# Retention with a gated feed-forward: transposing four chunks' activations by DMA, and a longer hand-ordered end

## The chip, the cores and the metric

The kernel runs on one core of a Trainium2 chip. The core has five engines with a queue each: TensorE (PE, matmuls; PEld is its weight load), VectorE (DVE), ScalarE (ACT), GpSimd (POOL) and SyncE (SP), which here issues nearly all transfers. An engine works its queue strictly in order; an instruction that waits keeps all behind it waiting. Sixteen DMA engines carry out the transfers. The metric is the device time of one execution in microseconds (us), lower being better. Three runs of the kernel before took 215.89, 216.18 and 216.53 us, a median of 216.18 us.

## The reference

Eight sequences of 576 positions with 8 heads of 64 go through a retention layer (attention with a decaying mask and no softmax), and the 4608 resulting rows of 512 through a feed-forward layer.

```python
scores = scale * np.matmul(q, k.transpose(0, 1, 3, 2))
ret = scores * Dmat[None]              # gamma_h ** (i - j) for i >= j, else 0
x = np.matmul(ret, v)                  # -> rows of 512
h = x @ w_in                           # 512 -> 1024
e = np.exp(h - h_max); sm = e / (e.sum(-1) + 1e-9)
solu = h * sm
ln = (solu - mu) / np.sqrt(var + 1e-6) * g_ln
out = ln @ w_out                       # 1024 -> 512
```

The inputs q, k, v and the weights are 32-bit; the kernel multiplies in 16-bit.

## The kernel before, in words

The work is cut into 36 chunks of 128 rows, numbered 0 to 35. Nine chunks belong to a pair of sequences: four chunks of 128 positions of each, alternating, and a last one (chunks 8, 17, 26 and 35) that holds the 64 remaining positions of both. From chunk to chunk of one sequence a state (keys times values, decayed) is carried, so the scores are only needed inside a chunk.

Each step of a chunk is a small function with a name of two letters:

- `ld` loads q, k and v of a chunk (three transfers on SyncE; six for chunks 8, 17, 26, 35). `cq`, `ck`, `cv` turn them into scaled 16-bit copies; the letter behind the chunk names the engine (a ScalarE, v VectorE, g GpSimd).
- q and k must be transposed for the scores. `tr` transposes on TensorE into a PSUM bank, and `er` copies the result out. From chunk 12 on, `tr` does only q (4 transposes), and `kd` has the keys transposed by a DMA on SyncE; the last chunks of the pairs are excepted (`chunks[n][1] == 4`): for them `kd` does nothing and `tr` transposes q and k (8 transposes, the group `tp`). `kq` transposes q by DMA, for one chunk.
- `sc` makes the scores (two banks), `mk` masks them on VectorE, `kv`, `ad`, `d3`, `dk` carry the state, `av` and `fs` make the retention output x, `ex` copies it out of PSUM.
- `m1` is the first projection (16-bit, eight matmuls of 512 columns, tile h), `mx` its row maximum (VectorE), `xp` the exponential (ScalarE), `so` the product u (VectorE), `sq` the sum of squares (ScalarE), `rt` the inverse root (three small POOL instructions).
- u must be transposed for the second projection. `tu` does this with eight transposes on TensorE into a bank (tile lp) and `eu` copies it out; `du` has a DMA do it instead, on SyncE, from SBUF to SBUF.
- `m2` is the second projection (eight matmuls of 512 columns, tile o), `st` scales its result on ScalarE and stores it through SyncE.
- The last chunk, 35, is done in halves by `hm`, `hx`, `hp`, `ho`, `ht`, `he`, `hq`, `h2`, `hw`.

The order of all queues is written out by hand, as lists of `step:chunk:engine`: START with absolute chunk numbers, LOOP relative to the loop's index i, END relative to chunk 35 (so `du:-7` is chunk 28). The steps are issued in the order of the lists, and each engine's queue is the order in which its steps occur there. LOOP runs for i from 7 to 27, and its steps reach from `tu`, `eu`, `sq`, `rt`, `m2`, `st` of chunk i-2 to `ld` of chunk i+6. A step that doesn't apply to its chunk does nothing.

`BANKS` names, for every PSUM tile that a step takes in turn, which of four banks it uses; two more pairs of banks hold h. SBUF tiles rotate over fixed numbers of buffers: five for u and for its transposed copy uT, four for qkT (the transposed q and k), seven for the loaded q and v, six for the loaded k.

So the program's order, the bank list and the buffer counts set when what can start; nothing is planned at run time.

Of the kernel before, what the change touches and what calls it, by code (L numbers as in the profile page):

```python
# [20 lines left out]
PLAIN = 5  # L21
FIRST = 7
STEP = 1
STOP = 28
BY_DMA = 12
START = """
ld:0 ld:1 c1:0 ck:0:g cq:0:v cv:0:v li:3 gt:0 c2:0 tq:0 cq:1:g cv:1:v ld:2 kv:0 ck:1:v tq:1 ad:0
# [17 lines left out]
ex:1:a rt:-2 cq:4:g xp:0 m2:-2 d3:0 ck:5:g st:-2 mk:2  # L45
"""
END = """
d3:-7 tr:-5 kd:-3 cq:-3:g kv:-6 av:-6 er:-5:v ld:-1 ad:-6 tr:-4 fs:-6 ex:-6:a dk:-7 sq:-9
so:-8 sc:-5 m1:-7 cv:-4:g er:-4:v mk:-5 tr:-3 kd:0 kv:-5 ck:-2:g av:-5 sq:-8 fs:-5 tu:-8 mx:-7
ad:-5 rt:-9 cv:-3:g dk:-5 er:-3:a tu:-9 kd:-2 m1:-6 xp:-7 sc:-4 kv:-4 cq:-2:v eu:-9:v so:-7  # L50
ex:-5:a m1:-5 sc:-3 mk:-4 rt:-8 du:-7 d3:-6 ld:0 mx:-6 eu:-8:a d3:-5 mk:-3 ad:-4 ck:-1:a dk:-6
m2:-9 av:-4 mx:-5 xp:-6 kv:-3 av:-3 d3:-4 cv:-1:g st:-9 d3:-1 ad:-3 kd:-1 cv:-2:g d3:-2 cq:0:g
fs:-4 fs:-3 so:-6 tr:-2 er:-2:v ex:-4:a xp:-5 m2:-8 sq:-6 dk:-4 sc:-2 mk:-2 ck:0:g m1:-4 so:-5
kv:-2 kv:-1 du:-5 ex:-3:a av:-2 sq:-7 st:-8 mx:-4 sq:-5 xp:-4 fs:-2 m1:-3 cq:-1:v cv:0:g kq:-1
rt:-5 dk:-3 ex:-2:a d3:-3 ad:-2 du:-6 tr:0 so:-4 er:0:a m2:-7 sc:0 m1:-2 ad:-1 mk:0 mx:-3
sc:-1 rt:-6 mk:-1 mx:-2 m2:-5 sq:-4 du:-4 kv:0 rt:-7 rt:-4 av:-1 av:0 fs:-1 dk:-1 m2:-6 st:-7
xp:-3 so:-3 ex:-1:v xp:-2 so:-2 du:-3 du:-2 dk:-2 sq:-3 st:-6 fs:0 m1:-1 rt:-3 ex:0:a st:-5
sq:-2 hm:0:0 hm:0:1 m2:-3 mx:-1 hx:0:0 hx:0:1 xp:-1 hp:0:1 so:-1 m2:-2 hp:0:0 ho:0:1 ho:0:0
du:-1 ht:0:1 hc:0 st:-3 ht:0:0 m2:-4 he:0:1:v sq:-1 hq:0:0:v he:0:0:v rt:-2 rt:-1 ad:0
hq:0:1:a h2:0:0 rt:0 m2:-1 h2:0:1 st:-4 st:-2 hw:0:0:a st:-1 hw:0:1:v  # L60
"""

BANKS = """
012312012012302130312031321320132103123120132130123012301230123012301230213021320132012301230213
021320132012301230213021320132013201321032103120312013201321032103120312013201321032103120312031
203102310210321032120312310213230213210213023201203203
"""


# [22 lines left out]
def kernel(  # L92
# [33 lines left out]
    chunks = []  # L126
# [4 lines left out]
    NCH = len(chunks)  # L131
# [29 lines left out]
    def bank(shape, dtype, name):  # L161
        return ps.tile(shape, dtype, tag="b" + next(banks), name=name)
# [4 lines left out]
    def copy(engine, out, in_):  # L167
        (engine.copy if engine is nc.scalar else engine.tensor_copy)(out=out, in_=in_)  # L168
# [32 lines left out]
    def tq(n):  # L201

        tp = bank([P, 2, 4, P], F16, "tp")
        for i, src in enumerate((T.pop(("q16", n)), T["k16", n])):
            s2 = src.rearrange("p h d -> p (h d)")
            for hp in range(4):
                nc.tensor.transpose(  # L207
                    out=tp[:, i, hp], in_=s2[:, hp * P : (hp + 1) * P], identity=ident
                )
        T["tp", n] = tp  # L210

    def kd(n):
        if chunks[n][1] == 4 or n < BY_DMA:
            return
        T["qkT", n] = att.tile([P, 2, 4, P], F16, name="qkT", bufs=4)
        nc.sync.dma_start_transpose(
            out=T["qkT", n][:, 1], in_=T["k16", n].rearrange("p h d -> p (h d)")
        )
# [4 lines left out]
        )  # L223

    def tr(n):
        if chunks[n][1] == 4 or n < BY_DMA:
            return tq(n)
        tp = bank([P, 4, P], F16, "tr")
        s2 = T.pop(("q16", n)).rearrange("p h d -> p (h d)")
        for hp in range(4):  # L230
            nc.tensor.transpose(  # L231
                out=tp[:, hp], in_=s2[:, hp * P : (hp + 1) * P], identity=ident
            )
        T["tp", n] = tp

    def er(n, e="a"):
        if chunks[n][1] == 4 or n < BY_DMA:
            return eq(n, e)
        copy(ENG[e], T["qkT", n][:, 0], T.pop(("tp", n)))

    def eq(n, e="v"):

        qkT = att.tile([P, 2, 4, P], F16, name="qkT", bufs=4)
        tp = T.pop(("tp", n))
        for i, x in enumerate(e if len(e) > 1 else ()):
            copy(ENG[x], qkT[:, i], tp[:, i])
        if len(e) == 1:
            copy(
                ENG[e], qkT.rearrange("p a b c -> p (a b c)"), tp.rearrange("p a b c -> p (a b c)")
            )  # L250
        T["qkT", n] = qkT
# [453 lines left out]
    def run(order, base):  # L705

        for token in order.split():
            name, n, *more = token.split(":")
            n = base + int(n)
            if 0 <= n < NCH:  # L710
                step[name](n, *more)

    with tc.manual_schedule():
        run(START, 0)
        for i in range(FIRST, STOP - STEP + 1, STEP):
            run(LOOP, i)
# [31 lines left out]
```

## Time and profile before

| What | Value |
|---|---|
| median of three runs | 216.18 us |
| profiled execution | 215.92 us, of which span 214.2 us |
| TensorE busy | 197.2 us (92%) |
| VectorE, ScalarE, GpSimd busy | 172.6, 166.3, 174.5 us |
| granted TensorE clock, mean | 0.998 |
| DMA | 47.04 MB, mean 220 GB/s |
| chain that ended last | PE 70%, DVE 12%, SPq 11% |

The span runs from the first to the last instruction; the time of an execution has some 1.7 us more. "SPq" in the chain is SyncE's queue. In the slices of the span a digit is the busy tenth of a fortieth of the span, some 5.4 us. The busy time of TensorE is modelled at the matmuls' ends, so a full TensorE is one that always has a matmul under way. Transfers are shown with their issue on SyncE (start and length) and, by group, with the time from issue to landing.

### The profile page before, as it was taken

Reading aid. Unit: us, or ns where it says so; the run is one execution under the profiler, and the core shown is the slowest. Engines: PE = TensorE matmul, PEld = TensorE weight load, DVE = VectorE, ACT = ScalarE, POOL = GpSimd, SP = SyncE. Lnnn points to the kernel's source line nnn. Section 1 sums busy time; section 2 is a strip of 40 time slices with the busy share of each in tenths; the row PEclk is TensorE's granted clock in tenths of the full one; section 3 lists DMA queues with packets and bytes.
Section 4 is the critical chain, followed back from the end, with each engine's and each line's share of the span. In section 5 each row is a group of like instructions: output and inputs, shape, how many; then the busy total and the mean of one; then the engine's idle time right before and its main releaser. Section 6 shows DMA issues by size and latency. Waiting matters only on the chain.

```text
span 214.2 us, 5359 instructions
## 1 busy us (share of the span) xinstructions
PE 197.2 (92%) x1989; PEld 110.5 (52%) x1989; DVE 172.6 (81%) x284; ACT 166.3 (78%) x269; POOL 174.5 (81%) x275
## 2 busy tenths in 40 slices
PE   1369888999999999999999999999999999999993
PEld 0244455555555555555555555555555565445451
DVE  1278999999997888888887888888878999879840
ACT  2073896989898888888888888888888776967991
POOL 3329799699997899999997899999988999897440
PEclk9999999999999999999999999999999999999999
DMA  7999999999999999899999999799999989792745
GB/s 148 258 291 292 195 221 355 232 187 229 275 282 247 257 200 197 180 254 242 240 224 232 244 206 198 177 258 232 232 227 227 238 170 206 168 196 78 196 115 180
DMA packets 139130, 47.04 MB, mean 220 GB/s; under 512 B 132824, under 2 KB 133088, under 8 KB 139104
## 3 DMA queue, kind: packets, MB, share of 16 engines
q1 hardware_dynamic: 138784, 46.55, 99.6%
q8 instruction: 15, 0.25, 0.5%
q10 hardware_dynamic: 320, 0.16, 0.4%
q14 instruction: 11, 0.09, 0.1%
HBM read 32.53 MB, written 9.44 MB: 196 GB/s over the span
## 4 chain that ended last, share of the span: by engine, by line
PE 70%; DVE 12%; SPq 11%; DMA 2%; issue 2%; POOL 1%; DVEq 0%; POOLq 0%
PE o L485 25%; PE h L382 22%; SPq L177 10%; PE lp L465 5%; PE sc L260 4%; PE x L350 3%; PE x L335 3%; PE kp L284 3%; DMA qf<-in_q_dram 2%; PE tr L231 2%; DVE u L407 2%; DVE nm L392 2%; DVE ret L273 2%; DVE w_c L700 2%; SPq L656 1%
## 5 line engine op out<-in xcount | busy, mean ns | idle before, releaser
L382 PE MATMUL h<-w_in,xT 128*128 128x512 f16 x264 | 62.4, 379 | 0.5 <-DVE u L407 0.5
L485 PE MATMUL o<-w_c,uT 128*128 128x512 f16 x240 | 56.5, 379 | 0.2
L398 ACT ACTIVATE e<-h,nm 128x1024 f32<-128x1024 f32 x35 | 39.0, 1116 | 11.5 <-DVE nm L392 11.5
L273 DVE TENSOR_TENSOR ret<-sc,tris 128x512 f16<-128x512 f32 x72 | 46.0, 680 | 1.3 <-PE sc L260 1.2
L407 DVE SCALAR_TENSOR_TENSOR u<-h,e 128x1024 f16<-128x1024 f32 x35 | 42.7, 1220 | 2.3 <-ACT e L398 0.9
L392 DVE TENSOR_REDUCE nm<-h 128x1 f32<-128x1024 f32 x35 | 42.4, 1214 | 2.1 <-PE h L382 2.0
L485 PEld LDWEIGHTS <-uT 128*128 128x128 f16 x280 | 26.2, 98 | 26.9
L382 PEld LDWEIGHTS <-xT 128*128 128x128 f16 x264 | 24.2, 98 | 24.5 <-issue 0.5
L184 POOL TENSOR_TENSOR v<-vf,small 128x512 f16<-128x512 f32 x32 | 33.4, 1044 | 3.4 <-DMA vf<-in_v_dram 3.4
L435 ACT ACTIVATE sq<-u,su 128x1024 bf16<-128x1024 f16 x30 | 34.7, 1158 | 0.2 <-DVE u L407 0.2
L184 POOL TENSOR_TENSOR q<-qf,small 128x512 f16<-128x512 f32 x30 | 31.8, 1061 | 3.5 <-DMA qf<-in_q_dram 3.5
L311 POOL TENSOR_TENSOR s<-t,small 128x512 f16<-128x512 f32 x32 | 33.8, 1058 | 0.0
L168 ACT CAST xT<-x 128x512 f16<-128x512 f32 x34 | 19.9, 586 | 11.4 <-PE x L350 10.9
L493 ACT ACTIVATE o_sb<-o,rs 128x512 f32<-128x512 f32 x35 | 23.9, 684 | 4.3 <-POOL rs L457 2.3
L168 ACT COPY uT<-lp 128x1024 f16<-128x1024 f16 x25 | 25.3, 1011 | 0.3 <-PE lp L465 0.2
L457 POOL TENSOR_TENSOR rs<-w,mhalf 128x1 f32<-128x1 f32 x36 | 19.9, 553 | 3.0
L168 POOL CAST k<-kf 128x512 f16<-128x512 f32 x28 | 17.4, 623 | 3.4 <-DMA kf<-in_k_dram 3.4
L299 DVE TENSOR_TENSOR t<-kp,s 128x256 f32<-128x256 f32 x24 | 10.1, 420 | 12.5 <-POOL s L311 10.2
L453 POOL TENSOR_SCALAR w<-ss,w 128x1 f32<-128x1 f32 x31 | 8.3, 267 | 14.1 <-ACT sq L435 11.8
L168 ACT COPY qkT<-tp 128x1024 f16<-128x1024 f16 x10 | 10.0, 1013 | 9.7 <-PE tp L207 9.7
L465 PE MATMUL lp<-ident,u 128*128 128x128 f16 x224 | 16.9, 219 | 0.7 <-DVE u L423 0.7
L323 POOL TENSOR_TENSOR s<-t,small 128x256 f32<-128x256 f32 x24 | 14.9, 621 | 2.6 <-DVE t L297 2.6
(88 smaller groups left out, 260.0 us busy)
## 6 DMA issues: line engine op xcount, KB each, us to landing
qf<-in_q_dram SPq DMA_DIRECT2D x32, 256.0 KB, 4.2
kf<-in_k_dram SPq DMA_DIRECT2D x32, 256.0 KB, 4.7
vf<-in_v_dram SPq DMA_DIRECT2D x32, 256.0 KB, 4.8
out_dram<-o_sb SPq DMA_DIRECT2D x32, 256.0 KB, 2.7
w_in<-in_moe_w_in_dram SPq DMA_DIRECT2D x4, 512.0 KB, 5.2
w_out<-in_moe_w_out_dram SPq DMA_DIRECT2D x4, 512.0 KB, 6.3
qf<-in_q_dram SPq DMA_DIRECT2D x8, 128.0 KB, 3.8
kf<-in_k_dram SPq DMA_DIRECT2D x8, 128.0 KB, 3.8
```

What stands on the lines that cost most here:

```text
L168: (engine.copy if engine is nc.scalar else engine.tensor_copy)(out=out, in_=in_)
L184: engine.tensor_tensor(out=dst, in0=T.pop((key, n)), in1=table.unsqueeze(2).to_broadcast([P, H, D]), op=ALU.mult,)
L273: nc.vector.tensor_tensor(out=r, in0=s, in1=m, op=ALU.mult)
L311: nc.gpsimd.tensor_tensor(out=s16, in0=t.unsqueeze(2).to_broadcast([P, 4, 2, D]), in1=gd.unsqueeze(3).to_broadcast([P, 4, 2, D]), op=ALU.mult,
L382: nc.tensor.matmul(out=h[:, i * 512 : (i + 1) * 512], lhsT=xT[:, d], rhs=w_in16[:, d, i * 512 : (i + 1) * 512], start=d == 0, stop=d == 3,)
L392: nc.vector.tensor_reduce(out=nm, in_=T["h", n], axis=AX.X, op=ALU.max, negate=True)
L398: nc.scalar.activation(out=e, in_=T["h", n], func=ACT.Exp, bias=T.pop(("nm", n)), accum_out=s)
L407: nc.vector.scalar_tensor_tensor(out=u, in0=T.pop(("h", n)), scalar=-1.0, in1=T.pop(("e", n)), op0=ALU.mult, op1=ALU.mult, accum_out=su,)
L435: nc.scalar.activation(out=s, in_=T.pop(("v", n)), func=ACT.Square, scale=-float(DFF), bias=T.pop(("su", n)), accum_out=ss,)
L465: nc.tensor.transpose(out=lp[:, c], in_=u[:, c * P : (c + 1) * P], identity=ident)
L485: nc.tensor.matmul(out=o, lhsT=uT[:, c], rhs=w[:, c], start=c == 0, stop=c == NF - 1)
L493: nc.scalar.activation(out=o_sb, in_=T.pop(("o", n)), func=ACT.Copy, scale=T.pop(("rs", n)))
```

## The change

LOOP stops at i = 23 instead of 27, and its four last passes become part of a new END. There, u of chunks 24 to 27 is transposed by `du` and no longer by `tu` and `eu`. The exception for the last chunks of the pairs shrinks to chunk 35, so that the keys of chunks 17 (in LOOP) and 26 are transposed by DMA too. The new END has another order on all engines: among other things the load of chunk 31 stands ahead of that of chunk 30, `er` of chunks 26 to 31 and 33 runs on ScalarE instead of VectorE, three `cv` go from GpSimd to VectorE, and two `ck` from GpSimd to ScalarE. BANKS is written anew to fit.

```diff
-STOP = 28
+STOP = 24
@@ END (the first and last lines of each; numbers relative to chunk 35)
-d3:-7 tr:-5 kd:-3 cq:-3:g kv:-6 av:-6 er:-5:v ld:-1 ad:-6 tr:-4 fs:-6 ex:-6:a dk:-7 sq:-9
...
-hq:0:1:a h2:0:0 rt:0 m2:-1 h2:0:1 st:-4 st:-2 hw:0:0:a st:-1 hw:0:1:v
+d3:-10 so:-12 cv:-8:g kd:-7 tu:-13 ld:-4 kv:-9 tr:-8 ad:-9 m1:-11 sq:-13 kv:-10 ad:-10 cq:-7:g
+tr:-9 eu:-13:a er:-8:a av:-10 fs:-10 dk:-10 er:-9:a mx:-11 tu:-12 sc:-9 mk:-9 ex:-10:a rt:-13
+cv:-7:g eu:-12:a xp:-11 kv:-8 m1:-10 sq:-12 ck:-6:a ad:-8 tr:-7 dk:-11 er:-7:a so:-11 sc:-8
+du:-11 m2:-13 av:-9 cv:-6:g ld:-5 sc:-7 mk:-8 fs:-9 mx:-10 cq:-4:g kd:-6 ck:-4:g m2:-12
+cq:-6:v st:-13 sq:-11 mk:-7 av:-8 ex:-9:a fs:-8 kd:-4 rt:-11 xp:-10 ex:-8:v cq:-5:g kv:-7
+so:-10 cv:-4:g tr:-6 m1:-9 er:-6:a ck:-5:a av:-7 rt:-12 d3:-8 m2:-11 m1:-8 mx:-9 cv:-5:g fs:-7
+sc:-6 xp:-9 kv:-6 dk:-8 ld:-3 kd:-5 tr:-5 ex:-7:a ad:-7 d3:-11 so:-9 dk:-7 mx:-8 st:-12
+cq:-3:g cv:-3:g st:-11 mk:-6 du:-10 m1:-7 er:-5:a ld:-2 ad:-6 av:-6 fs:-6 dk:-6 xp:-8 so:-8
+ex:-6:a du:-9 d3:-7 tr:-4 er:-4:a sc:-5 tr:-3 ck:-3:g mk:-5 mx:-7 m1:-6 mx:-6 sq:-10 kd:-3
+kv:-5 ld:-1 er:-3:a rt:-10 cq:-2:g av:-5 kv:-4 xp:-7 fs:-5 ad:-5 so:-7 ex:-5:a d3:-6 m2:-10
+sc:-4 ck:-2:g ad:-4 ad:0 m1:-5 du:-7 xp:-6 mk:-4 kd:-2 sq:-7 so:-6 tr:-2 dk:-5 av:-4 sq:-9
+kv:-3 er:-2:a d3:-5 du:-8 fs:-4 ad:-3 d3:-4 rt:-9 mx:-5 m2:-9 ld:0 ex:-4:a ck:-1:v cq:-1:g
...
+hw:0:0:v st:-1 hw:0:1:v
@@ in kd, tr and er alike
-        if chunks[n][1] == 4 or n < BY_DMA:
+        if n < BY_DMA or n == NCH - 1:
```

More of the change, by code (lines that the diff above doesn't have):

```diff
@@ L47 @@
 END = """
-d3:-7 tr:-5 kd:-3 cq:-3:g kv:-6 av:-6 er:-5:v ld:-1 ad:-6 tr:-4 fs:-6 ex:-6:a dk:-7 sq:-9
[L49 to L59, printed above, removed]
@@ new lines @@
+kv:-3 er:-2:a d3:-5 du:-8 fs:-4 ad:-3 d3:-4 rt:-9 mx:-5 m2:-9 ld:0 ex:-4:a ck:-1:v cq:-1:g
+sc:-3 sq:-6 kd:-1 mk:-3 sq:-8 kq:-1 cv:-1:v cv:-2:v xp:-5 d3:-3 m1:-4 m2:-7 rt:-7 dk:-4 st:-10
+rt:-8 sc:-2 mx:-4 du:-6 mk:-2 st:-9 m2:-8 av:-3 cq:0:g fs:-3 kv:-1 ck:0:g kv:-2 kd:0 dk:-3
+d3:-9 rt:-6 st:-7 xp:-4 av:-2 so:-5 fs:-2 tr:0 st:-8 ex:-3:a so:-4 du:-5 ex:-2:a ad:-2 er:0:a
+cv:0:v ad:-1 m1:-3 sq:-5 dk:-1 sc:0 mx:-3 sc:-1 mk:-1 m1:-2 rt:-5 dk:-9 sq:-4 m2:-6 mk:0 kv:0
+xp:-3 du:-4 av:0 mx:-2 so:-3 dk:-2 av:-1 fs:0 ex:0:a fs:-1 ex:-1:v du:-3 xp:-2 so:-2 m2:-5
@@ L61 @@
+sq:-3 m1:-1 st:-6 hm:0:0 hm:0:1 st:-5 mx:-1 sq:-2 rt:-2 m2:-4 xp:-1 hx:0:0 d3:-1 hx:0:1 hp:0:0
+m2:-3 so:-1 ho:0:0 hp:0:1 ho:0:1 du:-2 ht:0:0 rt:-3 ht:0:1 hc:0 m2:-2 du:-1 he:0:0:v rt:-4
+st:-4 hq:0:0:v hq:0:1:a he:0:1:v sq:-1 st:-2 rt:0 h2:0:0 m2:-1 d3:-2 st:-3 h2:0:1 rt:-1
+hw:0:0:v st:-1 hw:0:1:v
 """
 BANKS = """
-012312012012302130312031321320132103123120132130123012301230123012301230213021320132012301230213
-021320132012301230213021320132013201321032103120312013201321032103120312013201321032103120312031
@@ L66 @@
-203102310210321032120312310213230213210213023201203203
+012312012012302130312031321320132103123120132310323210321301230123012301320132031203123012301320
+132031203123012301320132031203120312032103210231023120312032103210231023120312031023120310231203
+23021330213021302102120203120312132020130123012012
 """
@@ L225, in tr @@
     def tr(n):
-        if chunks[n][1] == 4 or n < BY_DMA:
+        if n < BY_DMA or n == NCH - 1:
             return tq(n)
@@ L236, in er @@
     def er(n, e="a"):
-        if chunks[n][1] == 4 or n < BY_DMA:
+        if n < BY_DMA or n == NCH - 1:
             return eq(n, e)
```

## The prediction

> **What bounds the kernel now.** I read the page first: busy shares, slices, the chain that ended last.
>
> ```profile
> span 214.2 us, 5359 instructions
> PE 197.2 (92%) x1989; PEld 110.5 (52%) x1989; DVE 172.6 (81%) x284; ACT 166.3 (78%) x269; POOL 174.5 (81%) x275
> PE   1369888999999999999999999999999999999993
> PEclk9999999999999999999999999999999999999999
> DMA  7999999999999999899999999799999989792745
> q8 instruction: 15, 0.25, 0.5%
> PE 70%; DVE 12%; SPq 11%; DMA 2%; issue 2%; POOL 1%; DVEq 0%; POOLq 0%
> ```
>
> From 60 us to 210 us TensorE has no free slice, its granted clock is full, and the chain lies on it. So TensorE work that goes is time saved, as long as nothing else holds TensorE up. The chain in order of time gives the price of such work, and the end.
>
> ```profile
> 147.22 0.45 PE tp L207 x8
> 158.06 0.45 PE lp L465 x8
> 172.66 0.98 PE lp L465 x16
> 209.63 0.89 PE oh L589 x8
> ```
>
> Eight transposes are 0.45 us of TensorE; the last matmul ends at 210.52 us, and 3.7 us of eviction and store follow. The change lays work on SyncE's queue, so I read that queue in order of time.
>
> ```profile
> 151.07 0.43 SPq L177 DMA_DIRECT2D qf<-in_q_dram  x1
> 151.55 0.70 SPq L177 DMA_DIRECT2D kf<-in_k_dram  x1
> 152.29 1.03 SPq L177 DMA_DIRECT2D vf<-in_v_dram  x1
> 153.50 1.47 SPq L216 DMA_TRANSPOSE qkT<-k  x1
> 155.06 0.52 SPq L498 DMA_DIRECT2D out_dram<-o_sb  x1
> ...
> 156.96 2.30 SPq L177 DMA_DIRECT2D vf<-in_v_dram  x1
> ...
> 168.70 3.04 SPq L216 DMA_TRANSPOSE qkT<-k  x1
> 171.84 0.53 SPq L498 DMA_DIRECT2D out_dram<-o_sb  x1
> ...
> 177.52 1.25 SPq L470 DMA_TRANSPOSE uT<-u  x1
> 178.81 1.32 SPq L177 DMA_DIRECT2D qf<-in_q_dram  x2
> ```
>
> Columns are start, duration, instruction. One issue starts where the last ends: between 151 and 186 us SyncE waits for nobody, and its stores go out 1.5 to 2.9 us after ScalarE made them. SyncE is full, not only TensorE; its delay is hidden because loads run chunks ahead. The last view is of the engines that take what SyncE brings.
>
> ```profile
> 178.28 0.62 ACT L168 CAST k<-kf 128x512 f16<-128x512 f32 x1 [2.73 <-DMA kf<-in_k_dram]
> 183.99 1.04 POOL L184 TENSOR_TENSOR q<-qf,small 128x512 f16<-128x512 f32 x1 [0.95 <-DMA qf<-in_q_dram]
> 185.97 0.61 POOL L168 CAST k<-kf 128x512 f16<-128x512 f32 x1
> 188.27 0.39 PE L207 MATMUL tp<-ident,k 128*128 128x128 f16 x4
> ```
>
> The brackets are idle time. Only the loads of chunks 34 and 35 are placed by END now, and both were waited for. TensorE transposes chunk 35 (q from 188.05 us, then this k) 1.5 us after its keys were cast: that is all the slack left.
>
> **The change, part by part.** *TensorE.* Four `tu` go: 4 x 0.45 = 1.8 us. `tr` of chunks 17 and 26 halves: 2 x 0.22 = 0.44 us. Together -2.2 us, all on the path.
>
> *Other engines, behind the loop.* By row durations ScalarE loses three copies of `lp` (3 x 1.01) and one key cast (0.62), `ex` of 27 (0.58) and a half eviction (0.47), and takes seven `er` (7 x 0.57) and two key casts (1.24): +0.5 us. VectorE loses seven `er` (0.42 each, 0.69 for 26) and an `lp` copy (0.68), nets one `cq` less (0.69), and takes three `cv`, one `ck`, one `ex` and the half eviction: -0.9 us. POOL nets two `ck` and three `cv` less and one `cq` more: -3.3 us. All have 12 to 22% idle, and TensorE's 100% covers them. Uncovered, an `er` queued behind an exponential on ScalarE can keep the scores waiting: between 0 and 1.0 us (the exponential's own waits there are 0.8 to 0.9). I take 0, since the queue below is later than any of it.
>
> *SyncE.* Added: `kd` of 17 and 26, `du` of 24 to 27. From the start of chunk 30's load (151.07) to that of chunk 35's (178.81) the queue now issues 5 loads, 6 `kd`, 4 stores and 1 `du` in 27.74 us. Start to start these are: load 2.17 to 3.80 us, mean 2.62; `kd` 1.27 to 3.14, mean 1.83; store 0.60; `du` 1.29. The new order has, from `kd` of 28 to the load of 35: kd 28, ld 31, du 24, ld 30, kd 29, st 22, kd 31, ld 32, kd 30, st 23, st 24, du 25, ld 33, du 26, kd 32, ld 34, du 28, kd 33, du 27. That is 5 loads, 6 `kd`, 3 stores, 5 `du`: 27.74 - 0.60 + 4 x 1.29 = 32.3 us. It begins 1.55 us later, at 152.6, for `kd` of 26 now stands ahead of it. So the load of 35 starts at 184.9 us, not 178.8.
>
> What waits for it: the second half of q is issued 0.70 us later and needs 3.8 us to land (the page's median of such halves), then POOL scales q (1.04) and casts k (0.61): 191.1 us. `tr` of 35 needs both, and behind it on TensorE stand, in both orders, nine groups of eight 512-column matmuls and the same small ones; before, they took from 188.05 to 210.52. It moves by 191.1 - 188.05 = +3.0 us, and so does the end. The 2.2 us saved lie ahead of this wait and are eaten by it. TensorE is held up earlier on the same queue: `du` of 27 starts at 183.6 and lands 3.1 us later, 186.7; its `m2` (1.73) and six small groups (1.4) come before `tr` of 35, which puts that at 189.8, +1.8 by itself.
>
> *Ends.* Not shown before: how SyncE issues this mix. Shortest durations throughout (load 2.17, `kd` 1.27, store 0.56, `du` 1.29) bring the load of 35 at 178.9; middle ones (2.43, 1.55, 0.57, 1.29) at 182.3, +0.4 us; means, +3.0. Upward, `kd` of 17 also pushes SyncE by 1.55 us at 96 us; a transposed key lands 1.6 to 3.9 us before its scores in the loop, so TensorE does not feel it there, but what is left of the push at 151 us is between 0 and 1.55. I take the means, which are this queue's own under this load, and 0 for `kd` of 17, because the store's delay falls back to 0.5 to 0.8 us after each push by a six-transfer load.
>
> The long issues (2.30, 3.04) coincide with the 16 KB packets of the instruction queue, which start at 156.9 and 170.1 us; 180.5 and 193.6 follow. The Trainium skill ("Runtime: NRT & Kernel Launch", Instruction fetch mechanics) says crossing a 16 KiB block of instructions costs one DMA tail-bump, mostly hidden. By that no long issue belongs in the sum, and the middle durations' +0.4 us would hold; the trace has them on every such packet since 146 us, so I keep them.
>
> **Rivals.** *SyncE keeps up (faster).* If issues run near their shortest, the load of 35 starts before 181.2 us, POOL is done before TensorE gets there, and the saved transposes count: 216.18 - 2.2 = 214.0 us, up to 215.0 if the evictions on ScalarE bite. For it: 6.3 us of the old stretch (172.5 to 178.8) ran at 1.27, 2.17, 1.55, 1.29. Against: no stretch of 25 us did. It decides at the load of 35: started at 181.9, `tr` of 35 stands where it stood; each us is a us.
> The Trainium skill ("DMA: Bandwidth & Descriptors", Issuing engines are not separate DMA queues) says the sequencer's time to initiate a DMA is usually small relative to the DMA itself, by which four more would hardly delay the rest, and this rival's 214.0 would hold. Here a `du` holds SyncE 1.25 us of its 3.1.
>
> *A draw.* Middle durations, +0.4 us: 216.6, between 215.5 and 216.8. The long issues speak against it.
>
> *Worse (part of slower).* With `kd` of 17 still unabsorbed, +4.6: 220.8 us.
>
> **How the numbers follow.** The profiled execution took 215.92 us: span 214.2 and 1.7 around it, 0.26 below the median of 216.18. 214.2 + 3.0 + 1.7 = 218.9 on that footing, 219.2 on the median. Chances: forecast with its worse variant 0.67, draw 0.11, SyncE keeps up 0.22. 0.3% is 0.65 us, about what a measurement of this kernel can tell from no change; slower 0.67, same 0.11, faster 0.22. The forecast's own range is 216.9 to 221.2. The whole range reaches down to 214.8, inside the faster case, and leaves out the rest of it (0.13) and 0.05 above.
>
> **What would show it.** Right: on SyncE the load of chunk 35 starts after 182 us; POOL's `qf` wait before chunk 35 grows from 0.95 us; TensorE shows idle before `tp` of 35 and before `m2` of 27, its busy time down 2 us with the span up; ScalarE or POOL waits for chunk 30's load, which now stands behind chunk 31's. Wrong: that load starts before 181 us, or TensorE is solid to the end, and the span is near 212.

## The result, and the profile after

| What | Before | After |
|---|---|---|
| median | 216.09 us (4 executions) | 223.32 us (4 executions, 222.45 to 224.27) |
| ratio | 1 | 1.0333, 95% interval 1.0279 to 1.0386 |
| profiled execution, span | 215.92, 214.2 us | 223.94, 222.2 us |
| moved by DMA | 47.04 MB | 48.35 MB |

Ratios and intervals leave out executions more than 1.5% above the fastest one of their kernel.

The kernel became 7.2 us slower; the forecast was 3.0 us. The direction and the queue were as forecast, the size was not, and 223.32 lies above the range's 221.2. First the page of the changed kernel: span, busy shares, four rows of the slices, the instruction packets, the chain.

```profile
span 222.2 us, 5280 instructions
PE 196.8 (89%) x1949; PEld 108.4 (49%) x1949; DVE 173.3 (78%) x281; ACT 166.8 (75%) x272; POOL 171.7 (77%) x271
...
PE   1379889988999999999999999899997889997993
...
PEclk9999999999999999999999999999999999999999
DMA  7999999999999996999999896999999989789635
...
q8 instruction: 15, 0.25, 0.5%
...
PE 36%; SPq 16%; DMA 15%; POOL 14%; ACT 6%; DVE 6%; issue 6%; POOLq 0%; ACTq 0%
```

The 40 removed transposes are gone (1989 to 1949 matmul instructions), the clock is full, and no engine is busier than before by more than 0.7 us. But TensorE is no longer solid: the row of its slices has 8s and 7s in its last third, and its share of the chain fell from 70% to 36%. SyncE's queue and the DMAs took its place, 31% together. SyncE's queue in order of time, the rows that answer to those of before (start, duration, instruction):

```profile
154.93 1.23 SPq L224 DMA_TRANSPOSE qkT<-k  x1
...
158.40 3.48 SPq L478 DMA_TRANSPOSE uT<-u  x1
...
170.39 1.49 SPq L224 DMA_TRANSPOSE qkT<-k  x1
...
173.07 1.28 SPq L478 DMA_TRANSPOSE uT<-u  x1
...
178.01 2.10 SPq L478 DMA_TRANSPOSE uT<-u  x1
...
183.69 2.06 SPq L478 DMA_TRANSPOSE uT<-u  x1
...
187.12 1.30 SPq L478 DMA_TRANSPOSE uT<-u  x1
188.47 1.32 SPq L185 DMA_DIRECT2D qf<-in_q_dram  x2
```

The last row is the load of chunk 35: 188.47 us, where it was 178.81 before and 184.9 in the forecast. The five `uT<-u` rows are `du` of 24, 25, 26, 28 and 27; three of them held SyncE for 2.06 to 3.48 us, not 1.29. The key of chunk 30, at 170.39, went out at 164.02 before. Who waits for this, first GpSimd and ScalarE (their rows in order of time), then TensorE:

```profile
159.74 1.28 POOL L192 TENSOR_TENSOR q<-qf,small 128x512 f16<-128x512 f32 x1 [1.50 <-DMA qf<-in_q_dram]
...
165.57 1.04 POOL L192 TENSOR_TENSOR q<-qf,small 128x512 f16<-128x512 f32 x1 [2.75 <-DMA qf<-in_q_dram]
...
193.25 1.04 POOL L192 TENSOR_TENSOR q<-qf,small 128x512 f16<-128x512 f32 x1 [1.94 <-DMA qf<-in_q_dram]
```

```profile
166.78 0.62 ACT L176 CAST k<-kf 128x512 f16<-128x512 f32 x1 [3.72 <-DMA kf<-in_k_dram]
```

```profile
174.18 0.40 PE L268 MATMUL sc<-qkT 64*128 64x128 f16 x8 [0.95 <-DMA qkT<-k]
...
187.95 1.90 PE L493 MATMUL o<-w_c,uT 128*128 128x512 f16 x8 [0.48 <-DMA uT<-u]
...
194.35 0.40 PE L215 MATMUL tp<-ident,q 128*128 128x128 f16 x4 [0.34 <-POOL q L192]
194.91 0.40 PE L215 MATMUL tp<-ident,k 128*128 128x128 f16 x4 [0.16 <-POOL k L176]
...
204.00 1.90 PE L493 MATMUL o<-w_c,uT 128*128 128x512 f16 x8 [1.36 <-DMA uT<-u]
```

The brackets are idle time. The loads of chunks 31, 30 and 35 are waited for on GpSimd, that of chunk 30 also on ScalarE. TensorE starts chunk 35 at 194.35 us (188.05 before), 6.3 us later, and loses another 1.4 us at 204.00, before the second projection of chunk 30, whose `du` stands behind the late load in SyncE's queue. The last matmul ends at 218.45 us (210.50 before), 8.0 us later; some 1 us of this isn't the change's, for TensorE is 1.1 us late at 64 us already, where the two programs are alike.

Ahead of chunk 35 TensorE waited too. Its waits for transposed keys between 140 and 215 us (us in total, times, longest):

```profile
PE sc L268 <- DMA qkT<-k: 2.3, 4, 1.0
```

In all it idles 5.1 us between 140 us and the start of chunk 35, where the kernel before idles 0.1.

### The profile page after: what moved, and what is told of

It is laid out like the page before. It is cut to its first block, busy times and chain, and to the rows that moved or that the text cites. A ratio compares the mean times of both kernels' runs of the same rounds, so it can differ in the third digit from the quotient of the medians.

```text
span 222.2 us, 5280 instructions
## 1 busy us (share of the span) xinstructions
PE 196.8 (89%) x1949; PEld 108.4 (49%) x1949; DVE 173.3 (78%) x281; ACT 166.8 (75%) x272; POOL 171.7 (77%) x271
## 2 busy tenths in 40 slices
DMA packets 144442, 48.35 MB, mean 218 GB/s; under 512 B 138136, under 2 KB 138400, under 8 KB 144416
## 4 chain that ended last, share of the span: by engine, by line
PE 36%; SPq 16%; DMA 15%; POOL 14%; ACT 6%; DVE 6%; issue 6%; POOLq 0%; ACTq 0%
PE o L493 14%; SPq L185 11%; PE h L390 10%; DMA vf<-in_v_dram 4%; DMA w_out<-in_moe_w_out_dram 4%; DMA qf<-in_q_dram 3%; POOL q L192 3%; PE lp L473 2%; POOL v L192 2%; POOL s L319 2%; PE sc L268 2%; POOL k L176 2%; DMA uT<-u 2%; POOL rs L465 2%; ACT sq L443 2%
## 5 line engine op out<-in xcount | busy, mean ns | idle before, releaser
L192 POOL TENSOR_TENSOR q<-qf,small 128x512 f16<-128x512 f32 x31 | 32.6, 1050 | 10.2 <-DMA qf<-in_q_dram 10.1
L192 POOL TENSOR_TENSOR v<-vf,small 128x512 f16<-128x512 f32 x29 | 30.2, 1043 | 3.3 <-DMA vf<-in_v_dram 3.3
L176 ACT CAST xT<-x 128x512 f16<-128x512 f32 x33 | 19.3, 584 | 14.9 <-PE x L358 14.3
L176 ACT COPY uT<-lp 128x1024 f16<-128x1024 f16 x22 | 22.2, 1010 | 0.2 <-PE lp L473 0.2
L268 PE MATMUL sc<-qkT 64*128 64x128 f16 x288 | 15.2, 223 | 5.4 <-DMA qkT<-k 2.3
L176 POOL CAST k<-kf 128x512 f16<-128x512 f32 x26 | 16.2, 622 | 4.7 <-DMA kf<-in_k_dram 4.7
L176 ACT COPY qkT<-tp 128x1024 f16<-128x1024 f16 x10 | 10.0, 1012 | 10.3 <-PE tp L215 10.2
```

The lines of the kernel that those rows point to most:

```text
L192: engine.tensor_tensor(out=dst, in0=T.pop((key, n)), in1=table.unsqueeze(2).to_broadcast([P, H, D]), op=ALU.mult,)
```

## Experiments

Runs of one group shared a chip with executions of the kernel before. On those chips the kernel before took 219.0 to 219.8 us in the median, not 216.1, so ratios are compared, each to the kernel before on its own chip; 1% is 2.2 us. The kernel before was traced on the first chip only, so a time in a trace of these runs can't be held against its 178.81 us as it stands: ahead of their first edit the queue of `tiny_row` is 0.9 us late, that of `tiny_du` 2.4 us, and TensorE in `only_keys` is 5.0 us late at 74 us.

The theory to be tested: SyncE's issue time behind chunk 22 sets the loss (issue theory). Its rivals: the bytes that the transposes put on the DMA engines (bytes theory), the new order of the engines (order theory), and the two keys.

**The keys, alone and taken back.** `keys_by_pe` undoes the keys in the changed kernel, with the step `kv` of chunk 26, which issues no instruction, moved behind the `tr` that needs its keys; `only_keys` makes this edit alone on the kernel before.

```diff
@@ keys_by_pe, on the changed kernel (kd, tr, er)
-        if n < BY_DMA or n == NCH - 1:
+        if chunks[n][1] == 4 or n < BY_DMA:
@@ END
-... ld:-4 kv:-9 tr:-8 ... tr:-9 eu:-13:a
+... ld:-4 tr:-8 ... tr:-9 kv:-9 eu:-13:a
@@ only_keys, on the kernel before: the first edit reversed
```

> The changed kernel with the exception of the old one put back: the keys of chunks 17 and 26 are transposed by TensorE again (and the idle step kv of chunk 26 stands behind tr of 26). Theory 1, SyncE's queue is what is late: two issues of 1.55 us less on it; the hold-up of 0.9 us that the changed kernel shows on TensorE before the scores of chunk 24 goes, the load of chunk 35 starts 2 to 3 us earlier than 188.5, and the time falls from 223.3 to 220 to 221.5 us. Theory 2, the DMA engines' bytes: 0.26 of 48.35 MB less, so 222.5 to 223. Theory 3, the new order of the engines holds TensorE up by itself: 0.44 us more TensorE work, 223.3 to 223.8.

> The kernel before with only the keys of chunks 17 and 26 turned by DMA, in the old order. Theory 1, SyncE's queue: the push of chunk 17 is not absorbed, SyncE runs later and later behind it as in the changed kernel, TensorE is held up before the scores of some chunk from 20 on: 217 to 218.5 us. Theory 2, bytes: 216 to 216.5. Theory 3, only the order counts: 0.44 us of TensorE work less, 215.6.

Measured: `keys_by_pe` 1.0302 (1.0239 to 1.0366), `only_keys` 1.0128 (1.0063 to 1.0194). By the ratio two keys on SyncE cost 1.3% in a kernel that is otherwise as before, although they save 0.44 us of TensorE time. The trace doesn't show where: of its 6.0 us over the traced kernel before, 5.0 are there at 74 us, ahead of the first added key. And taking the keys out of the changed kernel gives next to nothing back (1.0302 beside 1.0333). The two prices do not add up to one sum; the keys are not the main cause.

**Fewer bytes per `du`, and `du` in the old order.** `small_du` has the DMA turn one block of 128 columns of u for chunks 24 to 27, and the second projection reads that block eight times. `du_old_order` is the kernel before, its order kept, with `du` of 24 to 26 behind the store of the chunk before.

```diff
@@ small_du, on the changed kernel
-        nc.sync.dma_start_transpose(out=uT, in_=T.pop(("u", n)))
+        u = T.pop(("u", n))
+        if n < 28:
+            nc.sync.dma_start_transpose(out=uT[:, 0:1], in_=u[:, 0:P])
+        else:
+            nc.sync.dma_start_transpose(out=uT, in_=u)
...
-                out=o, lhsT=uT[:, c], rhs=w[:, c], ...
+                out=o, lhsT=uT[:, 0 if 24 <= n < 28 else c], rhs=w[:, c], ...
@@ du_old_order, on the kernel before (tu and eu of 24 to 27 are skipped; du of 27 stands at tu)
     def st(n):
...
+        if 24 <= n + 1 < 27:
+            du(n + 1)
```

> The changed kernel, but du of chunks 24 to 27 moves only the first 128 of the 1024 columns of u, and m2 of these chunks reads that block eight times (their output rows are left wrong; TensorE's work is the same). As many issues on SyncE, 0.9 MB less for the DMA engines. Theory 1, the issue time on SyncE: 222 to 223.5 us, if an issue of an eighth still holds SyncE some 1.2 us. Theory 2, the bytes in the DMA engines: 4 x 0.9 us less, 219 to 220. Theory 3, the order: 223.3.

> The kernel before, old order, with tu and eu of chunks 24 to 27 replaced by du (of 24 to 26 on SyncE behind the store of the chunk before, of 27 where tu stood). TensorE has 1.8 us less to do. Theories 1 and 2, SyncE or the DMA engines are full: the loads and key transposes behind come 5.2 us (1) or 4 us (2) later, more than their slack of 1.5 to 2.6 us: 217 to 219.5 us. Theory 3, only the new order is at fault: 214.3 us.

Measured: `small_du` 1.0199 (1.0167 to 1.0232), `du_old_order` 1.0374 (1.0336 to 1.0413). With an eighth of the bytes 1.3 of 3.3 points come back. At the shortest an issue hardly gains from it. In its SyncE queue the four small ones took

```profile
159.25 1.47 SPq L480 DMA_TRANSPOSE uT<-u  x1
...
172.59 1.12 SPq L480 DMA_TRANSPOSE uT<-u  x1
...
176.90 1.76 SPq L480 DMA_TRANSPOSE uT<-u  x1
...
185.70 1.22 SPq L480 DMA_TRANSPOSE uT<-u  x1
```

But together they held SyncE 5.6 us, where the four of the changed kernel held it 8.2 us. So the run took away issue time along with bytes and can't tell the two apart; what is left of the loss, 2.0%, belongs to something else than these bytes. The old order does not help, but this run says less than it was made for. TensorE's waits (us in total, times, longest):

```profile
PE o L490 <- DMA uT<-u: 7.2, 2, 6.3
```

In this placement `du` of 25 stands in SyncE's queue behind the store of 24, which waits for the second projection of 24, which waits for `du` of 24: a serial chain, made by the experiment. The next group places `du` so that no store of its own chain stands ahead.

**Stores off SyncE; `du` placed well; issues without work.** `after_again` is the changed kernel unedited.

```diff
@@ after_st_act, on the changed kernel (st)
-            nc.sync.dma_start(out=out[...], in_=o_sb[pp])
+            eng = nc.scalar if n >= 22 else nc.sync
+            eng.dma_start(out=out[...], in_=o_sb[pp])
@@ du_behind_u, on the kernel before (tu and eu of 24 to 27 are skipped)
     def so(n):
...
+        if 24 <= n < 28:
+            du(n)
@@ tiny_du, on the kernel before (tu and eu stay)
+        if 24 <= n < 28:
+            tiny_t()
...
+    def tiny_t():
+        x = utp.tile([P, 1, P], F16, name="tt", bufs=1)
+        nc.sync.dma_start_transpose(out=x, in_=ident)
```

> The changed kernel itself, unedited, so that the next three stand beside it on one chip. Issue theory (SyncE's issue time behind chunk 22 sets the loss) and order theory (the new order of the engines loses by itself) alike: 3 to 3.5% over the kernel before, the load of chunk 35 issued 8 to 10 us later than in the kernel before, where SyncE starts it at 178.8 us.

> The changed kernel with the stores of chunks 22 to 35 issued by ScalarE, the engine that makes their rows, instead of SyncE: 14 stores of 0.5 to 0.6 us leave SyncE's queue, 3 to 5 of them ahead of the load of chunk 35. Bytes and the order of every other engine are the same. Issue theory: that load starts 2 to 3 us earlier than in the unedited changed kernel, and the time falls by 2 to 3 us, to 1 to 2% over the kernel before. Bytes theory (the loads are late because the transposes load the DMA engines) and order theory: the time stays within 0.7 us of the unedited changed kernel, or rises by up to 1 us from the issues that ScalarE now makes.

> The kernel before with its own order and its keys, but u of chunks 24 to 27 turned by DMA, each issued directly behind the instruction that makes u, so that no store stands ahead of it that waits for the same chunk (as one did in the run with the old order). Four transposes and evictions go, four DMA issues come; no instruction moves otherwise. Issue theory: 4 x 1.25 to 2 us are added to SyncE between 140 and 170 us, the load of chunk 35 starts 4 to 7 us later, its slack of 1.5 to 3 us is used up, and 1.8 us of TensorE time is saved in the stretch ahead of it: the time is 0.5 to 2% over the kernel before. Order theory: the transposes by DMA are harmless and save their 1.8 us: 0.5 to 1% under the kernel before.

> The kernel before, whole, with four extra DMA transposes of a constant 128 x 128 tile into scratch, issued at the same four places as in the run before this one. Nothing waits for them and they move 1/8 of the bytes; they only take SyncE's time (1.2 us each as in the run with the small transposes). Issue theory: nothing is saved and SyncE is pushed by 4 x 1.2 to 2 us: 0.5 to 2% over the kernel before, and the load of chunk 35 starts 4 to 7 us later. Bytes theory: within 0.3% of the kernel before.

Measured: `after_again` 1.0324 (1.0232 to 1.0415), `after_st_act` 1.0469 (1.0381 to 1.0557), `du_behind_u` 1.0254 (1.0170 to 1.0339), `tiny_du` 1.0255 (1.0175 to 1.0336). The order theory falls as the main cause: `du` of four chunks in the old order costs 2.5% by itself. The bytes theory falls as the whole cause: four transposes that nobody needs, of an eighth of the bytes, cost as much (they save TensorE nothing, where the four `du` save it 1.8 us, 0.8%). The issue theory missed at the stores: ScalarE issued them in 0.34 to 0.6 us each, yet the load of chunk 35 went out at 191.43 us, later than the 189.26 of `after_again`, and the time rose.

**Issue time apart from the transpose, and the four `du` left out.**

```diff
@@ tiny_copy, on tiny_du
-        nc.sync.dma_start_transpose(out=x, in_=ident)
+        for i in range(2):
+            nc.sync.dma_start(out=x[:, i], in_=ident)
@@ no_du, on the changed kernel (du)
+        if n < 28:
+            T.pop(("u", n))
+            T["uT", n] = w_out16[:, :, 0:P]
+            return
@@ swap, on du_behind_u (kd, tr, er)
-        if chunks[n][1] == 4 or n < BY_DMA:
+        if chunks[n][1] == 4 or n < BY_DMA or n in (28, 29, 30, 31):
@@ before_st_act: the edit of after_st_act on the kernel before
```

> The kernel before, whole, with eight extra plain DMA copies of the constant 128 x 128 tile into scratch, two at each of the four places where the run with the tiny transposes had one. Two copies hold SyncE about 1.1 us (0.5 us each, as its stores), nearly as long as one tiny transpose (1.2 us), and move twice its bytes. Issue theory (SyncE's time is what is lost): the loss of the run with the tiny transposes comes back, 1.5 to 2.5% over the kernel before, the load of chunk 35 issued 4 us later or more. Transpose theory (a DMA transpose holds up the DMA engines for some 1 us whatever its size, and SyncE's time is not what counts): within 0.7% of the kernel before.

> The changed kernel without the four DMA transposes of u of chunks 24 to 27: the second multiplication of these chunks reads a slice of the second weights in their place, so their output rows are wrong and nobody turns their u. Order, keys by DMA and all else stay. Theory that these four transposes are the loss: the load of chunk 35 starts 6 to 8 us earlier than in the unedited changed kernel, within 2 us of the kernel before, and the time is between 1% under the kernel before and 0.8% over it (the transposes of chunks 24 to 27 on TensorE, 1.8 us, are gone as well; what remains is the two keys' price). Order theory: at least 1.5% over the kernel before.

> The kernel before with u of chunks 24 to 27 turned by DMA behind the instruction that makes it (the run with 2.5% loss), and the keys of chunks 28 to 31, whose transposes stand in SyncE's queue at the same places, turned by TensorE instead. As many DMA transposes as in the kernel before; TensorE gives 1.8 us and takes 0.9 us; SyncE issues the same number of each kind; the bytes turned by DMA rise from 4 x 128 to 4 x 256 KB. Theory that the number of DMA transposes in this stretch is what costs (SyncE's issue or the DMA engines' pause, the same for each): the loss of 2.5% is gone, from 0.6% under to 0.6% over the kernel before. Bytes theory: a loss of 1 to 1.5% remains.

> The kernel before with the stores of chunks 22 to 35 issued by ScalarE. Control for the same edit in the changed kernel, which made that 1.4% slower instead of faster. If stores on ScalarE cost by themselves (a second queue at the DMA engines, or ScalarE's 14 issues): 1 to 2% over the kernel before here too. If they hurt only where SyncE's queue is overfull: within 0.5%. Issue theory with no cost of its own: 0 to 0.5% under.

Measured: `tiny_copy` 1.0119 (1.0025 to 1.0214), `no_du` 1.0041 (1.0001 to 1.0082), `swap` 0.9991 (0.9927 to 1.0056), `before_st_act` 1.0116 (1.0011 to 1.0220). Without the four `du` the changed kernel stands 0.4% over the kernel before: they are 2.8 of its 3.2 points, 6.2 us, 1.5 us each. `tiny_copy` lies between its two theories. `swap` looks like a success of "the number of transposes is what costs", but its single times ran from 218.5 to 226.2 us, with a median of 222.2 against 219.8, and the ratio rests on the low ones; it was left inconclusive and was repeated larger below. Stores on ScalarE cost 1.2% by themselves, by an interval that almost reaches 0, so their failure above does not speak against the issue theory alone; why they cost was not found.

**The same again, sharper.**

```diff
@@ tiny_row, on tiny_copy
-            nc.sync.dma_start(out=x[:, i], in_=ident)
+            nc.sync.dma_start(out=x[0:16, i], in_=ident[0:16])
@@ tiny_du_2: tiny_du unedited, for the same chip
@@ small_st, on the changed kernel (st)
+            w = 64 if 20 <= n <= 30 else DM
-            nc.sync.dma_start(out=out[rows, :], in_=o_sb[pp])
+            nc.sync.dma_start(out=out[rows, :w], in_=o_sb[pp, :w])
@@ no_du_no_keys: the edits of no_du and keys_by_pe together
```

> The kernel before, whole, with eight extra plain copies of 16 rows of the constant tile (4 KB each, 16 packets), two at each of the four places of the tiny transposes. SyncE's time as with the copies of 32 KB (about 0.5 us each), almost no work for the DMA engines. Issue theory: 0.7 to 2% over the kernel before, the load of chunk 35 issued 3 us later or more. Theory that the DMA engines hold SyncE back and its own time is slack: within 0.4% of the kernel before.

> The kernel before with the four tiny DMA transposes again, so that it stands beside the run with the 4 KB copies on one chip. 2 to 3% over the kernel before as it was. Issue theory: 0 to 0.7% above the run with the copies (4 x 1.2 us against 8 x 0.55 us of SyncE). Theory that a DMA transpose costs more than its issue: at least 1% above it.

> The changed kernel whose stores of chunks 20 to 30 write only the first 64 of 512 columns (the other columns of these rows stay unwritten): 11 stores of 32 KB in place of 256 KB, with as many issues. If the long issues (2 to 3.5 us where 1.25 is the shortest) are the DMA engines falling behind: issues of transposes after 155 us fall to 1.2 to 1.5 us, the load of chunk 35 starts 3 us earlier than in the unedited changed kernel, and the time falls to 1.5 to 2.5% over the kernel before. If SyncE's own time sets them: 2.8 to 3.5% over, as before.

> The changed kernel without the four DMA transposes of u of chunks 24 to 27 (their second multiplication reads a slice of the second weights instead, so these output rows are wrong) and with the keys of chunks 17 and 26 turned by TensorE as in the kernel before: what is left of the change is the order of the engines and 1.8 us less of TensorE. If the keys ate what was saved: 0.5 to 1% under the kernel before. If the new order costs by itself: 0 to 1% over.

Measured: `tiny_row` 1.0189 (1.0131 to 1.0248), `tiny_du_2` 1.0208 (1.0151 to 1.0265), `small_st` 1.0186 (1.0134 to 1.0238), `no_du_no_keys` 0.9962 (0.9914 to 1.0010). Eight copies of 4 KB, which nobody waits for, cost 1.9%, as much as the four transposes (`tiny_copy`, with eight times their bytes, had 1.2%; the intervals overlap): SyncE's time is what they share, and a place among the transfers under way. Their rows in the queue, and the load of chunk 35:

```profile
156.49 1.25 SPq L506 DMA_DIRECT2D tt<-ident  x2
...
163.46 1.16 SPq L506 DMA_DIRECT2D tt<-ident  x2
...
169.11 1.16 SPq L506 DMA_DIRECT2D tt<-ident  x2
...
179.09 1.51 SPq L506 DMA_DIRECT2D tt<-ident  x2
...
183.38 1.37 SPq L177 DMA_DIRECT2D qf<-in_q_dram  x2
```

That is 5.1 us of issues, and the load 4.6 us later than in the traced kernel before, 0.9 of which stood ahead of the first copy. The time is lost well ahead of that load, as TensorE's waits in this kernel say:

```profile
PE sc L260 <- DMA qkT<-k: 2.6, 1, 2.6
```

The scores of chunk 30 wait 2.6 us for a transposed key. The kernel before has no such wait: there this key lands at 168.01 us, 1.4 us ahead of its scores at 169.41; here it lands at 172.30.

The Trainium skill ("DMA: Bandwidth & Descriptors", Issuing engines are not separate DMA queues) calls the sequencer's time to initiate a DMA usually small relative to the DMA. The trace agrees for each of these copies, 0.5 to 0.9 us of issue against 2.0 to 4.2 us to its landing. Yet the eight, 5.1 us of such time for 32 KB, cost 1.9%: small isn't free in a queue that is full.

`small_st` kept every issue and took 11 x 224 KB off the DMA engines: 1.4 points less than the changed kernel's 3.2 to 3.3, although the load of chunk 35 moved only to 187.60 us and `du` of 24, 26 and 28 still held SyncE for 3.76, 1.89 and 2.12 us. So bytes cost too, here those of stores, and the long issues are not theirs alone. `no_du_no_keys` bounds the order: with TensorE's 1.8 us (0.8%) saved it is between 0.9% under and 0.1% over, so the order costs between nothing and 0.9%.

**The swap, larger.** u of 8 and of 14 chunks by DMA behind the instruction that makes it, and as many keys back on TensorE.

```diff
@@ swap_8, on swap
-        if 24 <= n < 28:
+        if 20 <= n < 28:
-        ... or n in (28, 29, 30, 31):
+        ... or 23 <= n < 32:
@@ swap_14: 14 <= n < 28, and 16 <= n < 32
```

> The kernel before with u of chunks 20 to 27 turned by DMA, each directly behind the instruction that makes it, and eight keys (chunks 23 to 31 without 26, whose keys TensorE turns anyhow) turned by TensorE instead: the same number of DMA transposes, 8 x 128 KB more moved, TensorE's work down by 8 x 0.22 = 1.8 us. If only the number of issues counts: 0.4 to 0.9% under the kernel before. If the bytes count too: 0.3 to 1.5% over.

> The same over 14 chunks: u of chunks 14 to 27 by DMA, fourteen keys of chunks 16 to 31 by TensorE, 14 x 128 KB more moved, TensorE's work down by 3.1 us. If only the number of issues counts: 0.8 to 1.4% under the kernel before. If the bytes count too: 0.5 to 3% over, and SyncE's issues of u between 80 and 150 us last clearly longer than 1.25 us.

Measured: `swap_8` 1.0152 (1.0079 to 1.0225), `swap_14` 1.0294 (1.0241 to 1.0347). The number of DMA transposes stayed and TensorE's work fell, so the number of issues alone is not the price. Counting the saved TensorE time, 5.1 and 9.5 us were lost for 1.05 and 1.84 MB more, 4.9 and 5.2 us per MB (3.4 to 6.4 and 4.6 to 5.8 by the intervals); at the page's mean of 220 GB/s a MB takes 4.5 us. That fits DMA engines without room. It isn't proof, for two other things changed: TensorE's waits for a transposed u also appear there (1.7 us in `swap_8`), and keys evicted with q are a larger copy. The expected long issues of u between 80 and 150 us did not come: 1.29 us in the mean of eight in `swap_14`.

No version tried was faster than the kernel before by more than can be measured.

## Why the prediction missed

*Right.* SyncE's queue is the place, and its delay arrives at the load of chunk 35 and `tr` of 35. The slack there was as forecast: the sum let 3.1 us of the push go unpaid (6.1 at the load, 3.0 at TensorE), and 3.4 us did (9.7 and 6.3). The load starts after 182 us, GpSimd's wait for its q grew from 0.95 to 1.94 us, TensorE idles before `tp` of 35, and ScalarE and GpSimd wait for chunk 30's load (3.72 and 2.75 us). TensorE's saving was eaten; the rival "SyncE keeps up" fell, and with it the draw. The wait ahead of `m2` of 27 came at `m2` of 28 (0.48 us). TensorE's busy time fell by 0.4 us, not 2, though all 40 transposes are gone.

*The step that failed* is the size of the push: "the load of 35 starts at 184.9 us". It started at 188.47, so the push was 9.7 us and not 6.1, and TensorE began chunk 35 6.3 us late, not 3.0. Another 1.7 us were lost behind that, where the sum had no term: 8.0 us at the last matmul.

The premise under the sum, "its delay is hidden because loads run chunks ahead", failed as well. It was checked at one place, the load of chunk 35. The keys in the same queue had less slack: the prediction notes 1.6 to 3.9 us between a key's landing and its scores, and used that for chunk 17 only; the key of chunk 30 had 1.4 us. In `tiny_row` TensorE is 0.2 us late at 142 us and 4.3 us at `tr` of 35, and 2.6 us of that is the wait for this one key. In the changed kernel TensorE, idling 5.1 us on the way, came to `tr` of 35 only 0.34 us before its q was ready: two paths of nearly the same length, of which the sum followed one.

*Terms that were mis-sized.*

- `kd` of 17 at 0. In the trace after, it held SyncE 2.64 us (at 97.17); before, the store at this place was held 2.26 us (at 96.20), each with a 16 KB packet of the instruction queue (97.43, 96.65). The queue was 0.8 us late ahead of it and 2.0 us behind it, so the key added 1.2 us, and on SyncE this was never absorbed: the queue was 3.4 us late at 140 us, and the stores of chunks 15, 18 and 20 went out 2.4, 6.2 and 4.2 us after ScalarE had made them, against 1.3, 3.7 and 0.8 before. TensorE did not feel it, as forecast: it was 0.9 us late at 137 us. The prediction had inferred from the store's delay falling back after a burst that SyncE would recover. The stretch from `kd` of 28 thus began at 154.93 us, not 152.6: 2.3 us, of which the first 0.8 stood ahead of this key and counts as scatter between executions. What the two keys cost in time is open: 1.3% alone (`only_keys`), 0.2 points in the full change (`keys_by_pe`), 0.8 between `no_du` and `no_du_no_keys`.
- `du` at 1.29 us. The five in the stretch took 10.2 us, not 6.5. Loads and keys came out shorter than their means, so the stretch took 33.5 us against 32.3: 1.2 us. Together with the late begin this is the whole difference at the load of chunk 35, 188.47 against 184.9.
- Nothing was set down for what stands behind that load. `du` of 29 and 30 do, and their `m2` waited 0.18 and 1.36 us; from `tr` of 35 to the last matmul it took 24.1 us, not 22.45.
- Nothing was set down for bytes. The prediction shows the row of DMA slices, nines in all but two slices from the second to the thirty-second, and reads nothing in it. The change adds 1.31 MB. `small_st` gains 1.4 points, about 3 us, with the same issues and with the four `du` holding SyncE 8.2 us, as in the changed kernel; `small_du` gains 1.3, but with 2.6 us less of issue time.

In the runs' own terms, the four `du` are 6.2 us of the 7.2 (`no_du`): with an eighth of their bytes some 3.4 us of them are left (`small_du` against `no_du`). How the 6.2 us divide between bytes and issues isn't shown, as the small ones also held SyncE 2.6 us less. What remains, order and keys less TensorE's saving, is 0.4%.

*The long issues* were kept in the sum with reason: those at 158.40 and 175.97 us (3.48 and 1.94) again hold a 16 KB packet of the instruction queue (160.10 and 176.39). But those at 178.01 and 183.69 (2.10 and 2.06) hold none; both are a `du` right behind a load. These two ended 0.75 and 0.82 us after the q load three transfers ahead had landed (179.36, 184.94). So the packets are at most half the story, and whether they or the landings cause any of it wasn't tried.

*Open.* Why an issue grows from 1.25 to 2 us and more, why stores cost more from ScalarE, and how issues and bytes share the price where both are added.

## What to carry over

When one in-order queue feeds several consumers, read the slack of every consumer, not only of the last: the tightest (here a transposed key with 1.4 us, against 3.1 at the last load) decides from where on each added issue is paid in full. A transfer has two prices, the time that it holds the issuing queue and the bytes on the DMA engines; where the queue's rows and the DMA slices both show no gap, count both, and even a 4 KB copy is not free. Work taken off an engine that is 92% busy is worth nothing if it goes to a queue that never stands still.

## What the runs showed of the hardware

- At its shortest, a DMA transpose holds SyncE about as long whatever its size: 1.12 us for 128 x 128 (`tiny_du`, `small_du`), 1.20 for keys of 128 x 512, 1.23 for u of 128 x 1024.
- An issue of a key in the kernel before lasts 1.21 to 3.04 us, and the end of many a longer one follows a landing: of those at 101.44, 111.72, 116.64 and 164.02 us the end came 0.45, 0.43, 0.15 and 0.25 us after the q load three transfers ahead had landed. Three transfers or four were under way at such times. That looks like SyncE being held until an earlier transfer is done; no run tested it.
- The Trainium skill ("Perfetto Trace Analysis", DMA Optimizations) says that spreading transfers over the engines that can issue them may help where making the descriptors is the bottleneck. Here issues on SyncE cost time, yet 14 stores moved to ScalarE made the kernel before 1.2% slower (0.1 to 2.2%) and the changed one 1.4% slower than it was (1.0469 against 1.0324).
